# ScalarE's table loads written out around the Mish pairs, with every time of the issue order laid out anew

## The chip, the cores and the metric

One NeuronCore of a Trainium2 chip runs the kernel in one launch. The metric is device time in microseconds from one run to the next, as the median over runs; a profiled execution shows every instruction on TensorE (PE; its weight loads PEld), VectorE (DVE), ScalarE (ACT), GpSimd (POOL) and SyncE's queue (SP).

## The reference

Attention within clusters, and a feed-forward network with Mish behind it. Cut to what matters:

```python
# q, k, v: (4, 8, 768, 64); centroids: (8, 16, 64); w_in: (512, 2048); w_out: (2048, 512)
q_assign = argmax(q_n . c_n); k_assign = argmax(k_n . c_n)        # nearest of 16 centroids, per head
scores = where(q_assign == k_assign, q @ k.T / 8, -1e9)
attn = softmax(scores) @ v                                        # exp, row sum, divide
x = attn as (3072, 512)
h = x @ w_in
sp = where(h > 20, h, log1p(exp(min(h, 20))))
out = (h * tanh(sp)) @ w_out                                      # h * tanh(softplus(h)) is Mish
```

## The kernel before, in words

**Units.** The attention runs in 96 units: 32 heads (4 batches of 8) times 3 blocks of 256 query rows, and a unit in two halves `a` of 128 rows. One half goes through `scores` (s: four matmuls into two PSUM banks; two such tiles exist, so the scores two halves later need the exponential that reads these banks), `rowmax` (m, DVE), `expo` (p, ACT, with the row sum l), `total` and `recip` (l), `p_hi` (hl, POOL), `p_lo` (hl, DVE), `ptrans` (pt, a DMA that transposes, issued on SP). Two units are a pair: `pv` multiplies their pt with the values (o), `pv_out` copies the result on ACT (x) and `x_lo` on DVE makes its low part. The first 24 units have a form of their own, with transposes on TensorE (q, pt) and without a second table; meanwhile both weights are loaded and prepared (`w_load`, `w_abs`, `w_low`, `w_f32`, `w_sq`, then `w_hi`, `w_lo`).

**FFN.** It follows the attention by 24 units. With every pair of units run two steps j of the first product: `m1` (h, 2 parts of 12 matmuls), `e_mish` (u, ACT), `e_gh` (g, POOL), `e_gl` (g, DVE), and, for the tile of 256 rows that is complete, steps `m2(k, a, f)` of the second product (O, six matmuls each; step f needs g of j = 8k + f), then `m_out` (osb, ACT) and `m_store`. The steps j from 80 on are done another way at the end, from some 770 us on; their order is not touched.

**Operands.** Each head's q and k are loaded on SP (`qk_load`), split on POOL (`prep_hi`, `prep_lo`: A, B), copied by DMA or ACT (`copy_t`, `copy_z`, `copy_b`, `copy_a`: T, Z), and assigned to clusters for four heads at a time (`assign_mm`, `assign_turn`, `assign_max`, `assign_hot`, `assign_back`, `assign_put`, `assign_stg`, `hot_copy`). `v_load`, `v_sq`, `v_high`, `v_split` do the like for the values.

**The order.** Nothing is scheduled by readiness: each engine works in the order in which the steps are issued. Every step has a time, in units, made from the tables `T` and `N`; `Plan.run` issues the steps by their times, and a step first issues those it names with `after` when they have not been issued. So a step can be pulled ahead of its own time. For the units behind the 24th and the FFN the times are:

```python
e = i // 2 * 2 + N["E"][i % 2 * 2 + a]
for key in ("scores", "rowmax", "expo", "total", "recip", "p_hi", "p_lo", "ptrans"):
    pl.at(e + N[key], ops[key], i, a)
...
pl.at(i + N["x_lo"] + 0.1 * (u - i), x_lo, u)          # u = i - 1 and i, i odd
...
t = ffn(j // 2 * 2)                                    # 23.993 + the even one of j
pl.at(t + N["m1"][j % 2 * 2 + fi], m1, j, fi)
for key in ("e_mish", "e_gh", "e_gl"):
    pl.at(t + N[key][j % 2], ops[key], j)
...
pl.at(ffn(8 * k + 4 * a + f / 2 + N["m2"][8 * a + f]), m2, k, a, f)
```

Below, e48_0 is the exponential of unit 48's half 0, s, m and p_lo likewise, and x46 the copy of unit 46's output.

**Tables.** ScalarE looks functions up in one table set at a time; the exponential and Mish are in different sets. At the start line 105 loads a set with the exponential and the logarithm by hand; every other load was put in by the builder, ahead of the first function that the loaded set lacks.

Of the kernel before, what the change touches and what calls it, by code (L numbers as in the profile page):

```python
# [26 lines left out]
class Plan:  # L27
# [9 lines left out]
        self.state = {}  # L37

    def at(self, t, fn, *args):
        self.ops[fn.__name__, *args] = (t, len(self.ops), fn, args)  # L40

    def issue(self, op):
        if op not in self.state:
# [28 lines left out]
def tile_clustered_attention_mish_ffn(  # L72
# [9 lines left out]
    nc = tc.nc  # L82
# [748 lines left out]
    def e_mish(j):  # L831
        pl.after(("m1", j, 0), ("m1", j, 1))
        if j % 2 == 0:
            st["g", j // 2] = gp.tile([P, 2, 2, 512], F16, tag="g2", name=f"g{j // 2}", bufs=4)
        st["u", j] = mp.tile([P, 512], F32, tag="u", name=f"u{j}")
        nc.scalar.activation(st["u", j], st["h", j], AF.Mish, scale=vst[j // 24, "h"])  # L836

    def e_gh(j):
        pl.after(("e_mish", j))
        nc.gpsimd.tensor_scalar(  # L840
            st["g", j // 2][:, j % 2, 0], st["u", j], vst[j // 24, "g"], 1.0,
            op0=ALU.mult, op1=ALU.mult,
        )
# [226 lines left out]
    def ffn(j):  # L1070

        return T["ffn"] + j

    ops = {
        fn.__name__: fn
        for fn in (scores, rowmax, expo, total, recip, p_hi, p_lo, ptrans, e_mish, e_gh, e_gl)
    }
    def start(i):

        return N["u"][i] if i < 24 else i  # L1080
# [37 lines left out]
    for q, n in owner.items():  # L1118
        if q == 0:
            continue  # L1120
        t = -12 if q == 0 else start(first[n]) + 3 * T["assign"]
# [15 lines left out]
    for n in range(32):  # L1137
        p = n // 16
        t = N["w"][n]
# [5 lines left out]
    for i in range(16):  # L1145
        t = N["ws"][i]
# [3 lines left out]
    def half(key, n, op):  # L1150
        i, a = divmod(T[key] + n, 2)
        if mode(i, a) == 3:
            return start(i) + T[op, a]
        return i // 2 * 2 + N["E"][i % 2 * 2 + a] + N[op]

    for p in range(2):
        t = half(("wh", p), 0, "scores")
# [3 lines left out]
    for b in range(2):  # L1161
        t = half(("vh", b), 0, "scores")
# [47 lines left out]
    for j in range(80):  # L1210
        t = ffn(j // 2 * 2)
# [4 lines left out]
    for k in range(9):  # L1216
        for a in range(2):
            for f in range(8):
                pl.at(ffn(8 * k + 4 * a + f / 2 + N["m2"][8 * a + f]), m2, k, a, f)
            t = ffn(8 * k + 4 * a + 3.5 + N["m2"][8 * a + 7])  # L1220
# [7 lines left out]
    for f in range(8):  # L1228
        for op in (c_whole, c_sums, c_high, c_low):
            pl.at(us(T["tail", "c"][f] + T["c", op.__name__]), op, f)  # L1230
        t = 7.84 * f
# [5 lines left out]
    for n in range(16):  # L1237
        a, f = divmod(n, 8)
        t = 3.92 * n + 2.62
# [33 lines left out]
    ('vh', 0): 5,  # L1273
    ('vh', 1): 45,
    'vh_step': 1,
    'v_sqd': -1.793,
    'cent_put': -17.25,
    'ffn': 23.993,
    'w_f': 0.331,
    'w_q': 0.827,  # L1280
    'w_lo': 0.305,
    ('z', 'prep_hi'): -17.4,
    ('z', 'prep_lo'): -15.2,
    ('z', 'copy_t'): -17.3,
    ('z', 'copy_a'): -15.0,
    ('z', 'copy_b'): -15.01,
    ('z', 'copy_z'): -15.1,
    ('z', 'assign_mm'): -15.0,
    ('z', 'assign_turn'): -15.05,
    ('z', 'assign_max'): -14.9,  # L1290
    ('z', 'assign_hot'): -14.8,
    ('z', 'assign_back'): -14.7,
    ('z', 'assign_put'): -14.6,
    ('z', 'hot_direct'): -14.55,
    ('z', 'assign_stg'): -14.4,
    ('z1', 'prep_hi'): -16.637,
    ('z1', 'copy_t'): 0.652,
    ('z1', 'prep_lo'): -0.394,
    ('z1', 'copy_z'): 0.103,
    ('z1', 'copy_b'): 0.753,  # L1300
    ('z1', 'copy_a'): 0.423,
    'as_turn': 1.351,
    'as_max': -0.357,
    'as_hot': 4.283,
    'as_back': 0.815,
    'as_put': 1.374,
    'as_stg': 1.508,
    'n_late': 9,
    'wide': 24,
    'v_s0': 36.614,  # L1310
    'act_q': 3,
    'xbufs': (5, 7, 4),
    'v_sq': 20.406,
    'assign': -1.297,
    'hot_copy': -0.251,
    'copy_a': -0.21,
    'copy_b': -0.38,
    'copy_z': -0.725,
    'copy_t': -0.806,
    'prep_lo': 1.071,  # L1320
    'prep_hi': 3.185,
    'load': -3.206,
    'raw': 4,
    ('f_ws', 0): 0,
    ('f_ws', 1): 1,
# [22 lines left out]
    ('f_b', 1): 1,  # L1348
    ('f_l', 0): 0.096,
    ('f_l', 1): 1,  # L1350
    ('w_l', 0): 2.19,
    ('w_l', 1): 1.226,
    'v0': -19.148,
    'v_d': -1.18,
    ('q_hi', 0): 2.631,
    ('q_lo', 0): 0.521,
    ('q_trans', 0): 0.78,
    ('q_hi', 1): 0.793,
    ('q_lo', 1): 3.324,
    ('q_trans', 1): 1.225,  # L1360
    ('f_w', 0): 1,
    ('f_w', 1): 0.659,
    'units0': 24,
# [5 lines left out]
    'O': 1,  # L1369
    ('ws1', 0): 2.668,  # L1370
    ('ws1', 1): -3.407,
    ('scores', 0): -0.068,
    ('rowmax', 0): -0.01,
    ('expo', 0): 0.345,
    ('recip', 0): 2.622,
    ('scores', 1): 0.349,
    ('rowmax', 1): 0.599,
    ('expo', 1): 6.966,
    ('recip', 1): 1.335,
    'pv': 1.42,  # L1380
    'pv_step': 0.487,
    'v_scale': 0.114,
    'pv_out': 2.609,
    ('w_s', 0): -0.341,
    ('w_s', 1): -0.361,
    ('f_sh', 0): 0.995,
    ('f_sh', 1): 1,
}


N = {
    ('load', 0): -7.458,
    ('load', 1): -10.096,
    ('load', 2): -6.974,
    ('load', 3): -4.979,
    'prep_hi': -3.418,
    'prep_lo': 0.494,
    'copy_t': -2.17,
    'copy_z': -2.427,
    'copy_a': -1.038,  # L1400
    'hot_copy': -2.049,
    'copy_b': -1.075,
    'assign_mm': -4.285,
    'assign_turn': -1.043,
    'assign_max': -4.058,
    'assign_hot': 0.071,
    'assign_back': -3.503,
    'assign_put': -0.183,
    'assign_stg': -2.372,
    'v_load': 16.573,  # L1410
    'v_sq': 18.112,
    'v_scale': 21.77,
    'v_max': 22.2,
    'v_pair': 10,
    'v_high': 26.705,
    'v_low': 27.262,
    'v_d': 2.046,
    'E': [0.355, 0.767, 1.154, 1.513],
    'scores': 2.166,
    'rowmax': -0.272,  # L1420
    'expo': -0.103,
    'total': 6.164,
    'recip': 0.144,
    'p_hi': 11.217,
    'p_lo': 1.549,
    'ptrans': 0.865,
    'pv': [5.55, 13.269, 7.015],
    'pv_out': 6.881,
    'x_lo': 2.789,
    'm1': [0.368, 0.616, 0.939, 1.346],  # L1430
    'e_mish': [4.782, 1.75],
    'e_gh': [1.685, 3.448],
    'e_gl': [1.743, 2.41],
    'm2': [4.854, 4.854, 4.854, 4.854, 4.854, 4.854, 4.854, 4.854, 4.881, 4.881, 4.881, 4.881, 4.881, 4.881, 4.881, 4.881],
    'm_out': -0.431,
    'm_store': 0.376,
# [3 lines left out]
}  # L1440


# [26 lines left out]
```

## Time and profile before

| | us |
|---|---|
| runs | 907.83, 908.76, 910.4 |
| their median | 908.76 |
| span of the profiled execution, first to last instruction | 908.0 |
| busy: PE / DVE / ACT / POOL | 850.7 / 701.2 / 516.8 / 416.9 |
| table loads on ACT: 1 at line 105, 35 at line 659 (exponential), 36 at line 836 (Mish) | 1.283 each |

For the profiled execution only its span is given; the runs' times are of other executions. Busy shares are averages over stretches with different limits. Matmuls overlap and their ends are modelled, so a busy PE is not PE at its peak; a wait of PE counts here only as the time in which it has no matmul at all.

### The profile page before, as it was taken

The page shows a single profiled execution, that of the slowest core. Times are in us where ns is not written, and L with a number is a line of the kernel's source. Part 1 is how long each engine was busy: PE and PEld are TensorE (multiplying, and loading weights), DVE is VectorE, ACT ScalarE, POOL GpSimd, SP SyncE. Part 2 cuts the span into 40 slices and gives each one's busy share as a digit, 9 for nine tenths or more (in the row PEclk, how much of TensorE's full clock was granted, in tenths as well). Part 3 has the DMA queues.
Part 4 walks back from the last instruction along what each step waited for, and adds up shares of the span by engine and source line. Part 5 has one row for each costly group of instructions (what it writes and reads, how often), then busy time and mean ns, then how long its engine had stood idle before and what let it go on. Part 6 is the DMA issues. An engine that isn't in the chain of part 4 may idle for free.

```text
span 908.0 us, 17381 instructions
## 1 busy us (share of the span) xinstructions
PE 850.7 (94%) x6671; PEld 611.1 (67%) x6671; DVE 701.2 (77%) x1178; ACT 516.8 (57%) x876; POOL 416.9 (46%) x410
## 2 busy tenths in 40 slices
PE   7899788869999999899999999999999999999998
PEld 3666565656667666677667667667667676677787
DVE  7879978777897769788987689699887776378841
ACT  6767867655556565556565666556556565145520
POOL 1443638565556445456555455466555544110000
PEclk9999999999999999999999999999999999999999
DMA  8645582258677796679779787679587675200001
GB/s 326 209 142 161 161 243 59 48 100 170 127 152 156 145 241 117 116 159 182 142 136 173 186 178 144 121 152 197 113 137 150 140 143 93 48 12 12 2 19 41
DMA packets 253058, 121.49 MB, mean 134 GB/s; under 512 B 230288, under 2 KB 230800, under 8 KB 252976
## 3 DMA queue, kind: packets, MB, share of 16 engines
q1 hardware_dynamic: 247632, 108.46, 54.4%
q10 hardware_dynamic: 5344, 11.93, 6.2%
q8 instruction: 52, 0.85, 0.4%
q14 instruction: 30, 0.25, 0.1%
HBM read 35.72 MB, written 6.29 MB: 46 GB/s over the span
## 4 chain that ended last, share of the span: by engine, by line
PE 48%; DVE 22%; issue 9%; ACT 8%; POOL 7%; DMA 5%; ACTq 0%; SPq 0%; POOLq 0%; DVEq 0%
DVE m L647 6%; PE o L750 6%; PE h L827 5%; DVE hl L714 5%; PE h L828 5%; PE h L829 5%; PE s L630 4%; PE O L864 4%; PE O L866 4%; PE O L865 4%; PE s L635 4%; DVE g L848 4%; ACT p L659 3%; POOL g L840 2%; DMA pt<-hl 2%
## 5 line engine op out<-in xcount | busy, mean ns | idle before, releaser
L659 ACT ACTIVATE p<-s,m 128x768 f32<-128x768 f32 x192 | 173.0, 901 | 116.6 <-DVE l L671 89.9
L697 POOL TENSOR_SCALAR hl<-p,l 128x768 f16<-128x768 f32 x144 | 160.2, 1117 | 123.9 <-DVE l L679 43.3
L647 DVE TENSOR_REDUCE m<-s 128x1 f32<-128x768 f32 x192 | 182.4, 950 | 32.2 <-PE s L635 28.8
L714 DVE SCALAR_TENSOR_TENSOR hl<-p,l,hl 128x768 f16<-128x768 f32 x144 | 181.2, 1259 | 8.6 <-POOL hl L697 8.2
L827 PE MATMUL h<-x,w 128*128 128x256 f16 x640 | 176.9, 276 | 3.8 <-ACT u L836 3.6
L828 PE MATMUL h<-x,w 128*128 128x256 f16 x640 | 175.5, 274 | 0.0
L829 PE MATMUL h<-x,w 128*128 128x256 f16 x640 | 175.5, 274 | 0.0
L630 PE MATMUL s<-A,B 128*128 128x384 f32 x384 | 122.0, 399 | 19.9 <-ACT p L659 14.7
L840 POOL TENSOR_SCALAR g<-u,mscg 128x512 f16<-128x512 f32 x80 | 72.5, 906 | 143.6 <-ACT u L836 135.3
L866 PE MATMUL O<-w,g 128*128 128x512 f16 x320 | 121.4, 379 | 7.6 <-DVE g L848 7.6
L864 PE MATMUL O<-w,g 128*128 128x512 f16 x320 | 121.8, 381 | 2.8 <-POOL g L840 2.7
L865 PE MATMUL O<-w,g 128*128 128x512 f16 x320 | 121.3, 379 | 0.0
L635 PE MATMUL s<-Z,T 80*128 80x384 f32 x384 | 100.1, 342 | 0.7 <-DMA T<-stg 0.6
L827 PEld LDWEIGHTS <-w 128*128 128x128 f16 x768 | 75.5, 98 | 32.5 <-issue 21.8
L630 PEld LDWEIGHTS s<-A,B 128*128 128x128 f32 x384 | 62.9, 191 | 44.0 <-ACT p L659 24.3
L848 DVE SCALAR_TENSOR_TENSOR g<-u,mscg,g 128x512 f16<-128x512 f32 x80 | 83.9, 1049 | 9.2 <-POOL g L840 6.8
L659 ACT ACT_TABLE_LOAD x35 | 44.9, 1283 | 79.3 <-DVE m L647 72.1
L828 PEld LDWEIGHTS <-w 128*128 128x128 f16 x768 | 75.9, 99 | 14.9 <-issue 4.2
L829 PEld LDWEIGHTS <-w 128*128 128x128 f16 x768 | 75.5, 98 | 9.0
L750 PE MATMUL o<-pt,v 128*64 128x256 f16 x1296 | 78.1, 274 | 0.5 <-DVE l L671 0.5
L750 PEld LDWEIGHTS <-v 128*64 128x64 f16 x1296 | 67.7, 110 | 15.7 <-issue 12.4
L635 PEld LDWEIGHTS s<-Z,T 80*128 80x128 f32 x384 | 70.2, 190 | 1.5 <-DMA T<-stg 0.9
(225 smaller groups left out, 1311.5 us busy)
## 6 DMA issues: line engine op xcount, KB each, us to landing
qk<-in_qk_dram SPq DMA_DIRECT2D x32, 384.0 KB, 5.0
stage<-in_w_in_dram SPq DMA_DIRECT2D x16, 512.0 KB, 7.6
stage<-in_w_out_dram SPq DMA_DIRECT2D x16, 512.0 KB, 5.1
vraw<-in_vP_dram SPq DMA_DIRECT2D x16, 384.0 KB, 6.5
T<-A ACTq DMA_DIRECT2D x30, 192.0 KB, 3.2
Z<-B SPq DMA_DIRECT2D x30, 192.0 KB, 3.3
B<-T ACTq DMA_DIRECT2D x28, 192.0 KB, 3.7
out_dram<-osb SPq DMA_DIRECT2D x20, 256.0 KB, 4.4
```

The lines of the kernel that those rows point to most:

```text
L630: nc.tensor.matmul(s[:, j, :384], st["B", n][:, q0 : q0 + P], st["A", n][:, j * 384 : (j + 1) * 384], start=True, stop=False,)
L635: nc.tensor.matmul(s[:, j, :384], st["T", n][: D + NCL, q0 : q0 + P], st["Z", n][: D + NCL, j * 384 : (j + 1) * 384], start=False, stop=True,)
L647: nc.vector.tensor_reduce(m, st["s", i, a][:, :, :384], axis=AX.XY, op=ALU.max, negate=True)
L659: nc.scalar.activation(p.rearrange("p (n x) -> p n x", n=2), st["s", i, a][:, :, :384], AF.Exp, bias=st["m", i, a], scale=1.0, accum_out=l,)
L697: nc.gpsimd.tensor_scalar(t[:, 0], p, r, 1.0, op0=ALU.mult, op1=ALU.mult)
L714: nc.vector.scalar_tensor_tensor(t[:, 1], p, r, t[:, 0], op0=ALU.mult, op1=ALU.subtract)
L750: nc.tensor.matmul(o[s * D : s * D + D, :256], v if early else v[:, int(part == 1)], st["pt", 2 * m + s][:, :, c + (0 if early or part < 2 ...
L827: nc.tensor.matmul(o, wh, xh, start=(c == 0), stop=False)
L828: nc.tensor.matmul(o, wh, xl, start=False, stop=False)
L829: nc.tensor.matmul(o, wl, xh, start=False, stop=(c == 3))
L864: nc.tensor.matmul(o, gh, wh, start=(f == 0 and fi == 0), stop=False)
L866: nc.tensor.matmul(o, gl, wh, start=False, stop=(f == 7 and fi == 1))
```

## The change

`e_mish` gets two loads written out: Mish's set ahead of the first Mish of a pair, and the exponential's set behind the second one, for j below 72. `Plan.at` can add a shift to a step's time, from a table `SHIFT` that is empty. Nearly all times in `T` and `N` are new; no computation is added or left out. The diff, with the lists `u`, `w` and `ws` and most of `T` left out:

```diff
     def at(self, t, fn, *args):
-        self.ops[fn.__name__, *args] = (t, len(self.ops), fn, args)
+        op = fn.__name__, *args
+        self.ops[op] = (t + SHIFT.get(op, 0), len(self.ops), fn, args)
...
         st["u", j] = mp.tile([P, 512], F32, tag="u", name=f"u{j}")
+        if j % 2 == 0:
+            nc.scalar.preload_act_table_set("mish")
         nc.scalar.activation(st["u", j], st["h", j], AF.Mish, scale=vst[j // 24, "h"])
+        if j % 2 and j < 72:
+            nc.scalar.preload_act_table_set("natural_log_exp_and_others")
...
-    ('w_l', 0): 2.19,
-    ('w_l', 1): 1.226,
+    ('w_l', 0): 3.03,
+    ('w_l', 1): 0.965,
...
 N = {
-    ('load', 0): -7.458,
-    ('load', 1): -10.096,
-    ('load', 2): -6.974,
-    ('load', 3): -4.979,
-    'prep_hi': -3.418,
-    'prep_lo': 0.494,
-    'copy_t': -2.17,
-    'copy_z': -2.427,
+    ('load', 0): -9.013,
+    ('load', 1): -10.835,
+    ('load', 2): -6.827,
+    ('load', 3): -5.085,
+    'prep_hi': -3.572,
+    'prep_lo': 1.216,
+    'copy_t': -2.829,
+    'copy_z': -2.24,
...
-    'E': [0.355, 0.767, 1.154, 1.513],
-    'scores': 2.166,
-    'rowmax': -0.272,
-    'expo': -0.103,
-    'total': 6.164,
-    'recip': 0.144,
-    'p_hi': 11.217,
-    'p_lo': 1.549,
-    'ptrans': 0.865,
-    'pv': [5.55, 13.269, 7.015],
-    'pv_out': 6.881,
-    'x_lo': 2.789,
-    'm1': [0.368, 0.616, 0.939, 1.346],
-    'e_mish': [4.782, 1.75],
-    'e_gh': [1.685, 3.448],
-    'e_gl': [1.743, 2.41],
-    'm2': [4.854, 4.854, 4.854, 4.854, 4.854, 4.854, 4.854, 4.854, 4.881, 4.881, 4.881, 4.881, 4.881, 4.881, 4.881, 4.881],
-    'm_out': -0.431,
-    'm_store': 0.376,
+    'E': [0.382, 0.808, 1.235, 1.505],
+    'scores': 0.582,
+    'rowmax': -0.28,
+    'expo': 4.085,
+    'total': 9.597,
+    'recip': 0.209,
+    'p_hi': 11.057,
+    'p_lo': 1.167,
+    'ptrans': 0.814,
+    'pv': [6.978, 19.207, 5.531],
+    'pv_out': 8.853,
+    'x_lo': 2.778,
+    'm1': [0.136, 0.893, 1.132, 1.575],
+    'e_mish': [6.744, 1.671],
+    'e_gh': [1.774, 2.299],
+    'e_gl': [1.667, 2.915],
+    'm2': [4.545, 6.49, 7.882, 4.714, 5.842, 6.227, 6.493, 4.761, 4.932, 5.145, 5.769, 4.636, 4.154, 4.821, 7.994, 4.844],
+    'm_out': -0.422,
+    'm_store': 0.914,
...
+SHIFT = {
...
+}
```

## Rows read from the trace of the kernel before

**Rows 1.** Busy time by stretch: PE, PEld, DVE, ACT, POOL, then clock, DMA share, GB/s

```profile
0.00:187.00 187.00, 159.78 (x1169) 109.89 (x1170) 153.06 (x284) 131.06 (x253) 85.75 (x105) 0.99 0.55 166
187.00:240.00 53.00, 43.06 (x340) 31.89 (x342) 42.67 (x67) 29.53 (x48) 33.52 (x31) 0.94 0.75 146
240.00:770.00 530.00, 513.80 (x4072) 363.89 (x4064) 429.78 (x700) 307.64 (x501) 289.34 (x265) 1.00 0.76 150
770.00:908.00 138.00, 134.03 (x1096) 105.42 (x1096) 75.69 (x128) 48.55 (x76) 8.33 (x11) 1.00 0.08 22
```

**Rows 2.** PE's waits from 240 to 770: us in total, times, longest us

```profile
PE O L866 <- DVE g L848: 7.1, 14, 0.9
PE s L630 <- ACT p L659: 5.4, 8, 1.5
PE O L864 <- POOL g L840: 2.7, 4, 0.8
```

**Rows 3.** PE's waits from 187 to 240

```profile
PE s L630 <- ACT p L659: 6.9, 3, 4.3
PE h L827 <- ACT u L836: 3.0, 1, 3.0
```

**Rows 4.** ACT's groups, 240 to 770: busy us, mean ns | idle before, its releasers

```profile
L659 ACT ACTIVATE p<-s,m 128x768 f32<-128x768 f32 x128 | 115.2, 900 | 98.2 <-DVE l L671 81.4 <-DVE m L647 15.1
L836 ACT ACTIVATE u<-h,msch 128x512 f32<-128x512 f32 x65 | 44.3, 682 | 0.7
L659 ACT ACT_TABLE_LOAD x32 | 41.1, 1283 | 66.9 <-DVE m L647 59.7 <-DVE vsm L398 7.2
L836 ACT ACT_TABLE_LOAD x32 | 41.1, 1283 | 0.6
```

**Rows 5.** ACT's timeline in one pair: start us, us, instruction [idle before]

```profile
473.84 0.38 ACT L787 ACTIVATE x<-o 64x256 f16<-64x256 f32 x1 [0.66 <-PE o L750]
...
478.24 1.28 ACT L659 ACT_TABLE_LOAD   x1 [1.05 <-DVE m L647]
```

**Rows 6.** The chain of waits, 463 to 490: start us, us, what

```profile
463.73 1.28 ACT L659
465.02 1.00 ACT p L659 x2
466.07 0.62 PE s L630 x2
...
467.27 0.11 PE h L829
...
468.36 0.35 PE s L630 x2
...
471.69 2.09 PE o L750 x36
...
474.09 0.21 PE O L865
...
487.16 2.09 PE o L750 x36
```

**Rows 7.** DVE's groups, 240 to 770

```profile
L714 DVE SCALAR_TENSOR_TENSOR hl<-p,l,hl 128x768 f16<-128x768 f32 x128 | 160.4, 1253 | 6.3 <-POOL hl L697 6.0
L647 DVE TENSOR_REDUCE m<-s 128x1 f32<-128x768 f32 x128 | 121.7, 951 | 21.9 <-PE s L635 21.0
L848 DVE SCALAR_TENSOR_TENSOR g<-u,mscg,g 128x512 f16<-128x512 f32 x66 | 70.8, 1073 | 2.1
L811 DVE SCALAR_TENSOR_TENSOR x<-o,x 64x256 f16<-64x256 f32 x52 | 22.0, 422 | 48.5 <-ACT x L787 47.4
```

**Rows 8.** ACT's waits from 120 to 132: us in total, times, longest us

```profile
ACT pt L728 <- DMA Z<-B: 3.1, 1, 3.1
```

**Rows 9.** The tile pt, 200 to 770: its DMAs, issue to landing

```profile
DMA to landing us min/median/max: 3.6/3.9/8.0
```

**Rows 10.** ACT's groups over the whole span: the load at line 105

```profile
L105 ACT ACT_TABLE_LOAD x1 | 1.3, 1283 | 1.7 <-PEq L1459 1.7
```

More of the change, by code (lines that the diff above doesn't have):

```diff
@@ L1275 @@
     'vh_step': 1,
-    'v_sqd': -1.793,
-    'cent_put': -17.25,
+    'v_sqd': -5.865,
+    'cent_put': -16.698,
     'ffn': 23.993,
-    'w_f': 0.331,
+    'w_f': 0.342,
     'w_q': 0.827,
[L1281 to L1307, printed above, removed]
+    'w_lo': 0.312,
+    ('z', 'prep_hi'): -17.672,
+    ('z', 'prep_lo'): -12.698,
+    ('z', 'copy_t'): -15.888,
+    ('z', 'copy_a'): -14.732,
+    ('z', 'copy_b'): -14.765,
+    ('z', 'copy_z'): -16.337,
+    ('z', 'assign_mm'): -11.552,
+    ('z', 'assign_turn'): -14.554,
+    ('z', 'assign_max'): -16.003,
+    ('z', 'assign_hot'): -13.258,
+    ('z', 'assign_back'): -12.666,
+    ('z', 'assign_put'): -12.998,
+    ('z', 'hot_direct'): -6.027,
+    ('z', 'assign_stg'): -14.77,
+    ('z1', 'prep_hi'): -15.822,
+    ('z1', 'copy_t'): -0.562,
+    ('z1', 'prep_lo'): -2.335,
+    ('z1', 'copy_z'): 2.134,
+    ('z1', 'copy_b'): 2.571,
+    ('z1', 'copy_a'): 1.339,
+    'as_turn': 2.548,
+    'as_max': -0.442,
+    'as_hot': 2.486,
+    'as_back': 0.39,
+    'as_put': 0.846,
+    'as_stg': 1.187,
     'n_late': 9,
     'wide': 24,
-    'v_s0': 36.614,
+    'v_s0': 36.503,
     'act_q': 3,
     'xbufs': (5, 7, 4),
[L1313 to L1322, printed above, removed]
+    'v_sq': 20.248,
+    'assign': -1.284,
+    'hot_copy': -0.423,
+    'copy_a': -0.208,
+    'copy_b': -0.408,
+    'copy_z': -0.702,
+    'copy_t': -0.829,
+    'prep_lo': 0.852,
+    'prep_hi': 0.614,
+    'load': -4.519,
     'raw': 4,
@@ L1350 @@
     ('f_l', 1): 1,
-    ('w_l', 0): 2.19,
-    ('w_l', 1): 1.226,
[L1353 to L1360, printed above, removed]
+    ('w_l', 0): 3.03,
+    ('w_l', 1): 0.965,
+    'v0': -18.341,
+    'v_d': -5.322,
+    ('q_hi', 0): 4.355,
+    ('q_lo', 0): 0.677,
+    ('q_trans', 0): 0.738,
+    ('q_hi', 1): 0.764,
+    ('q_lo', 1): 4.007,
+    ('q_trans', 1): 1.215,
     ('f_w', 0): 1,
@@ L1371 @@
     ('ws1', 1): -3.407,
[L1372 to L1376, printed above, removed]
+    ('scores', 0): -0.149,
+    ('rowmax', 0): 0.082,
+    ('expo', 0): 0.31,
+    ('recip', 0): 3.8,
+    ('scores', 1): 0.364,
     ('rowmax', 1): 0.599,
[L1378 to L1381, printed above, removed]
+    ('expo', 1): 3.986,
+    ('recip', 1): 1.374,
+    'pv': 1.419,
+    'pv_step': 0.48,
     'v_scale': 0.114,
-    'pv_out': 2.609,
-    ('w_s', 0): -0.341,
-    ('w_s', 1): -0.361,
+    'pv_out': 2.608,
+    ('w_s', 0): 0.187,
+    ('w_s', 1): -0.515,
     ('f_sh', 0): 0.995,
@@ L1391 @@
 N = {
-    ('load', 0): -7.458,
-    ('load', 1): -10.096,
-    ('load', 2): -6.974,
-    ('load', 3): -4.979,
-    'prep_hi': -3.418,
-    'prep_lo': 0.494,
-    'copy_t': -2.17,
-    'copy_z': -2.427,
[L1400 to L1411, printed above, removed]
+    ('load', 0): -9.013,
@@ L1412 @@
+    ('load', 1): -10.835,
[5 more added lines that the diff above has]
+    'copy_z': -2.24,
+    'copy_a': -2.094,
+    'hot_copy': -1.531,
+    'copy_b': -0.948,
+    'assign_mm': -4.206,
+    'assign_turn': -3.351,
+    'assign_max': -3.982,
+    'assign_hot': 1.536,
+    'assign_back': -3.3,
+    'assign_put': 0.576,
+    'assign_stg': -2.392,
+    'v_load': 17.344,
+    'v_sq': 18.153,
     'v_scale': 21.77,
-    'v_max': 22.2,
+    'v_max': 21.48,
@@ L1414 @@
     'v_pair': 10,
-    'v_high': 26.705,
-    'v_low': 27.262,
-    'v_d': 2.046,
-    'E': [0.355, 0.767, 1.154, 1.513],
-    'scores': 2.166,
-    'rowmax': -0.272,
-    'expo': -0.103,
-    'total': 6.164,
-    'recip': 0.144,
-    'p_hi': 11.217,
-    'p_lo': 1.549,
-    'ptrans': 0.865,
-    'pv': [5.55, 13.269, 7.015],
-    'pv_out': 6.881,
-    'x_lo': 2.789,
-    'm1': [0.368, 0.616, 0.939, 1.346],
-    'e_mish': [4.782, 1.75],
-    'e_gh': [1.685, 3.448],
-    'e_gl': [1.743, 2.41],
-    'm2': [4.854, 4.854, 4.854, 4.854, 4.854, 4.854, 4.854, 4.854, 4.881, 4.881, 4.881, 4.881, 4.881, 4.881, 4.881, 4.881],
@@ L1435 @@
-    'm_out': -0.431,
-    'm_store': 0.376,
[3 rows of a table removed]
+    'v_high': 26.765,
+    'v_low': 27.613,
+    'v_d': 3.411,
+    'E': [0.382, 0.808, 1.235, 1.505],
[14 more added lines that the diff above has]
+    'e_gl': [1.667, 2.915],
```

6 rows, old and new, of the table N are left out of this document.

## The prediction

> **What bounds the kernel now.** I read the busy time by stretch first, cut at the first Mish load (187 us), at 240 and at 770, where the last pairs of units end [rows 1]. From 240 to 770 TensorE is busy 513.80 of 530.00 us with a granted clock of 1.00, while DVE has 429.78 and ScalarE 307.64: TensorE is the bound, and 16.2 us is what its idle time can give back. From 187 to 240 it idles 9.94 us of 53, before 187 it idles 27.2 us, after 770 only 4.0.
>
> Then TensorE's own waits. Between 240 and 770 they are 5.4 us of scores waiting for an exponential (8 times), and 7.1 + 2.7 us of the second FFN product waiting for g [rows 2]. Between 187 and 240 they are 6.9 us for three exponentials and 3.0 us for a Mish [rows 3].
>
> Then ScalarE. From 240 to 770 it loads a table 64 times at 1283 ns: 32 times for the exponential (line 659), with 66.9 us of idle time ahead of them, and 32 times for Mish (line 836), with 0.6 us ahead [rows 4]. So the exponential's load stands behind its instruction's wait for the row maximum: at 478.24 ScalarE has idled 1.05 us for m, and only then loads [rows 5]. The Mish's load does not wait for the matmul that its Mish waits for; it costs 1.28 us between an exponential and a Mish. The chain of waits shows the price where it counts: load at 463.73, exponential at 465.02, and the scores that need that exponential's banks start at 466.07 [rows 6].
>
> **The exponential's load behind the second Mish.** It waits for nothing there, so it leaves the path m, load, exponential. It saves the smaller of 1.28 us and the idle time in front of it: 66.9 / 32 is 2.1 us on average, so nearly always the whole 1.28. Mish's load written out stays where it was, behind an exponential. Five loads are added: Mish's for the four pairs from j = 72 on (three of them with no exponential between), and an exponential's behind the pair before. They are 5 x 1.283 = 6.4 us of ScalarE, at or after the last exponential, where it is busy 48.55 of 138 us [rows 1]: I cost them at nothing, and at 6.4 us if that cover were gone.
>
> The order around them decides the rest. I worked it out from the times and from what each step pulls forward. For a pair of units 48, 49 (Mish 24, 25) ScalarE had: e48_0, e48_1, e49_0, e49_1, load, Mish, x46, Mish, x47, load, e50_0. It gets: e48_0, e48_1, e49_0, load, Mish, Mish, load, x46, e49_1, x47, e50_0. So the Mish pair and both loads move ahead of the pair's fourth exponential, and that exponential moves behind the copy x46, which waits for the pair's P·V product.
>
> From the end of P·V to the end of e50_0, before: x 0.38, x_lo 0.42, g 1.07, x_lo 0.42, p_lo 1.25, row maximum 0.95, load 1.28, exponential 1.00, in all 6.77 [rows 4 to 7]. The trace agrees: P·V ends at 471.69 + 2.09 = 473.78, and the load at 478.24 puts the exponential's end at 480.54. After: x 0.38, e49_1 1.00, x 0.38, x_lo 0.42, p_lo 1.25, row maximum 0.95, exponential 1.00, in all 5.38; g now stands ahead of x_lo, where P·V covers it. So e50_0 ends 1.4 us sooner against P·V.
>
> What queues behind. The second load ends 0.68 + 1.28 = 1.96 us after the second Mish's matmuls. TensorE has P·V's 2.09 us behind these, in one pair of four also one FFN step of 6 x 0.215 = 1.3 us: the copy x46 has 0.1 or 1.4 us to spare, and where an earlier exponential was late, it starts late. The fourth exponential ends 1.38 us after P·V; the scores that take its banks start 2.0 us after P·V at the soonest (scores 4 x 0.17, then 12 x 0.11) [rows 6]. Its p_lo stood behind the next row maximum and still does, so the transposes go out about when they did: that p_lo starts 4.5 us after P·V before, 4.4 after. On SyncE's queue loads of q and k move ahead of some transposes; each waits for a buffer that, by the order, an earlier step has freed. GpSimd gets the odd g ahead of the fourth p_hi, 0.7 to 1.4 us of work that ends before that exponential does.
>
> TensorE's order is less even: the FFN steps in four pairs were 3, 5, 3, 5 and are 1, 7, 2, 6, several of them right behind P·V. A pair's third scores come 5.3 us after P·V in the shortest kind (9 of 36), 7.9 or more in the others; they need e50_0 at 5.38. Before they came about 8.0 after, against 6.77. So three kinds of four gain spare time, and the shortest has none.
>
> **Sum, 240 to 770.** The 5.4 us of scores: seven of the eight waits follow a loaded exponential and are (5.4 - 1.5) / 7 = 0.56 us on average, less than the 1.28 taken out; the eighth, 1.5 us, has the odd g ahead of a row maximum on DVE, and that g moves behind it. All 5.4; the bounds are 0 and 5.4. The 9.8 us for g: Mish is one exponential (1.00) sooner, and two more FFN steps (2.6 us) lie ahead of the ones that waited, but the odd g now stands behind e49_1 and the second x: 0.38 + 1.00 + 0.38 + 0.42 + 1.07 = 3.25 us after P·V against 3.9 for its matmul. If the load is a microsecond late, it waits again. I take two thirds, 6.5; the bounds are 0 and 9.8. New waits in the shortest pairs: half a microsecond in some, 2. Together 9.9.
>
> **187 to 240.** Pairs without second products are shorter than the loop, so each of three waits loses up to 1.28: about 3.0 of 6.9 [rows 3]. The Mish that TensorE waits 3.0 us for is one exponential sooner, 1.0. Together 4.0. The granted clock is 0.94 here, a mean over both levels [rows 1]; what shorter waits give back of it is at most 0.06 x 53 = 3.2, and I count nothing.
>
> **Before 187.** No table is loaded there; the moves are many and small. One has a row: ScalarE waits 3.1 us for Z<-B [rows 8], a transfer queued on SyncE behind four weight loads, and now behind three. I take 2.4. The bounds are a loss of 5 and a gain of 8, about a fifth and a third of the idle 27.2.
>
> 9.9 + 4.0 + 2.4 = 16.3. The profiled span is 908.0, and the median of the runs is 0.8 above it: 908.8 - 16.3 = 892.5. Waits are counted as idle time only, and a matmul's end is modelled late (they start 0.11 us apart, rows 6, while each counts as longer), so the true loss is a little larger: 891.
>
> A load is one row of 1283 ns, and in the trace before, 32 Mish loads have 0.6 us of idle time ahead of them in all [rows 4], and at 463.73 + 1.28 the exponential follows its load at once [rows 6]: two written loads cost 2.57 us and no more. The Trainium skill, page "ScalarE: Activation LUTs", section "What ACT_TABLE_LOAD costs", states the same 1283 ns and adds a drain of about 1380 ns to every switch. The trace agrees with the load and shows no room for the drain; by it the two loads of a pair would hold ScalarE 2.76 us longer.
>
> **Rivals.**
> Only the load leaves the path, and the moves give and take alike: seven waits, 3.9 us, and 3.0 from 187 to 240, so 902. For it: 9.8 us of the gain hang on g, whose order changes both ways. Against: e50_0 gains on the whole loop.
>
> No change: TensorE, 97% busy from 240 to 770, hides the loads, and the early moves lose what the loads gain: 906 to 911. Against it stand the waits of rows 2 and 3.
>
> Slower: the fourth exponential now depends on P·V, so P·V, exponential, p_hi, p_lo, transposes, next P·V become one loop: 0.38 + 1.00 + 0.38 + 0.42 + 1.25 + 0.95 + 1.25 = 5.63, a transpose's landing 3.9 (at most 8.0) [rows 9], P·V 2.09, in all 11.6. Half of the pairs shrink to 14.0 us between P·V products (15.47 before: 471.69 to 487.16) [rows 6]. From a landing above 6.3 us the next product is late, and the lateness is handed on. At 1.5 us in 18 pairs this is 27 us, so 891 + 27 = 918. For it: landings reach 8.0. Against: the median is 3.9.
>
> Loads that cost double, because each must wait for what ScalarE has under way: priced at one more load row each, 2.57 us for the two, x46 is 2.57 - 0.1 = 2.5 us late in the short pairs. The 9 shortest have nothing to spare and lose it: 22 us, so 891 + 22 = 913. Rows 4 and 6 speak against it. The skill's drain, named above, is this case; its own figure would give 2.76 - 0.1 = 2.7 in 9 pairs, about 915.
>
> The builder adds its own loads to the written ones: then the exponential pays 1.28 again, and the time is 905 to 912. Against it: the load at line 105 is written out, and line 187's exponential has no load of its own [rows 10].
>
> **Numbers.** Forecast 0.62 (range 879 to 898); only the load 0.16; no change 0.07; slower by the loop 0.11; loads that cost double 0.02; loads added twice 0.02. The forecast's lower end takes back all 25.1 us of rows 2 and 3, the 2.4 and the clock's 3.2, less a microsecond: 879. Its upper end is g at 0 gain: 898. For 8 in 10 the range goes up to 908, through the second case and half of the third. Faster by over 0.3% (what a measurement of this kernel can tell from no change) 0.79, within it 0.08, slower 0.13.
>
> **What would show it.** Right: no idle time ending in a load at an exponential; two loads per pair around two neighbouring Mish; PE's waits on exponentials from 240 to 770 under 1 us; waits on g at most 4; the stretch between two P·V products uneven, 14 to 18 us, with a mean under 15.6. Wrong: P·V waiting for a transpose, x46 starting a microsecond or more behind P·V's end, the first scores after Mish waiting for the fourth exponential, or an early part that ends later than 187.

## The result, and the profile after

The changed kernel takes 881.25 us (median of 4 runs, 878.82 to 882.74) beside 909.18 for the kernel before (907.83 to 910.40): a ratio of 0.9685, 95% interval 0.9658 to 0.9711. Run again beside the last experiments it took 879.21 (6 runs, 877.55 to 880.75), 0.9662 [0.9636, 0.9687]. It is faster by 28 to 30 us, where 18 were forecast; the time lies in the forecast's range.

To see where the time came from, both traces have to be cut at the same work, not at the same microsecond. I cut them where the exponential of the first half of units 24, 30 and 90 starts. These are landmarks on ScalarE; on TensorE, whose order changed, up to 31 matmuls fall on another side of them. Busy time by stretch, cut there, first before and then after; the columns are those of [rows 1].

```profile
0.00:175.24 175.24, 148.15 (x1075) 101.25 (x1076) 145.74 (x271) 124.79 (x242) 82.01 (x103) 0.99 0.56 172
175.24:231.12 55.88, 46.23 (x352) 34.32 (x352) 43.35 (x67) 29.80 (x48) 34.18 (x31) 0.94 0.62 121
231.12:725.68 494.56, 479.30 (x3804) 339.44 (x3803) 405.21 (x657) 287.66 (x469) 273.49 (x249) 1.00 0.77 154
725.68:908.00 182.32, 176.99 (x1443) 136.08 (x1441) 106.90 (x186) 74.54 (x119) 27.26 (x28) 1.00 0.22 47
```

```profile
0.00:166.37 166.37, 145.71 (x1084) 100.19 (x1086) 145.60 (x270) 124.66 (x243) 77.85 (x101) 1.00 0.60 183
166.37:212.56 46.19, 39.49 (x321) 29.23 (x322) 39.26 (x65) 29.72 (x48) 36.53 (x32) 1.00 0.74 142
212.56:696.09 483.53, 480.88 (x3820) 342.69 (x3819) 406.98 (x659) 286.57 (x468) 293.75 (x251) 1.00 0.82 157
696.09:878.40 182.31, 177.66 (x1449) 136.98 (x1447) 109.67 (x186) 80.99 (x124) 27.94 (x29) 1.00 0.23 47
```

The four stretches shrink by 8.9, 9.7, 11.0 and 0.0 us, in all 29.6. In each, the stretch's length less TensorE's busy time (the two figures behind the stretch's bounds) is TensorE's idle time: it falls from 27.1 to 20.7, from 9.7 to 6.7, from 15.3 to 2.7, and from 5.3 to 4.7, by 22.7 in all. The other 6.9 us are busy time, for the same matmuls (6671 in the first trace, 6670 in the second). Most of it goes between units 24 and 30, where each matmul is shorter at the higher clock and 31 fewer fall. These 31 lie in the other stretches now; at the 0.13 us of busy time that one has there before (46.23 / 352), some 4 of that stretch's 9.7 us moved and weren't saved.

TensorE's waits after, from 220 to 740 us (total, times, longest), against [rows 2]. The second FFN product never waits for g any more, and two waits for an exponential are left of eight:

```profile
PE s L631 <- ACT p L660: 1.5, 2, 1.0
PE o L751 <- DMA pt<-hl: 0.7, 1, 0.7
PE as L543 <- DMA qk<-in_qk_dram: 0.2, 1, 0.2
```

The two waits for an exponential have a new cause. Both exponentials stand behind a cast on ScalarE (line 512) that waits for a transfer; from 240 to 770 us before, that cast has only 0.4 us of idle time ahead of it. ScalarE's waits over the same stretch have:

```profile
ACT A L512 <- DMA T<-A: 6.7, 2, 3.7
```

ScalarE's groups over the same stretch, against [rows 4]. The exponential's load (line 841) now has 0.6 us of idle time ahead of it in all, where it had 66.9: it no longer stands behind a wait.

```profile
L660 ACT ACTIVATE p<-s,m 128x768 f32<-128x768 f32 x129 | 115.9, 898 | 140.0 <-DVE l L672 71.5 <-DVE m L648 68.2
L839 ACT ACTIVATE u<-h,msch 128x512 f32<-128x512 f32 x66 | 42.6, 685 | 4.0 <-PE h L830 3.6
L841 ACT ACT_TABLE_LOAD x33 | 42.3, 1283 | 0.6
L838 ACT ACT_TABLE_LOAD x32 | 41.1, 1283 | 0.6
```

One pair on ScalarE's timeline, against [rows 5]. By the count of exponentials it is the pair of units 58 and 59, as there; x46, x47 and e50_0 name the places in the order. In the chain of waits its P·V product is the row `448.03 2.09 PE o L751 x36`, so it ends at 450.12. Load, two Mish and load lie ahead of that, x46 starts 0.06 us behind it, the fourth exponential and x47 follow, and e50_0 starts at 454.77, behind its row maximum alone.

```profile
445.48 1.28 ACT L838 ACT_TABLE_LOAD   x1
446.77 0.69 ACT L839 ACTIVATE u<-h,msch 128x512 f32<-128x512 f32 x1
448.06 0.69 ACT L839 ACTIVATE u<-h,msch 128x512 f32<-128x512 f32 x1 [0.60 <-PE h L830]
448.77 1.28 ACT L841 ACT_TABLE_LOAD   x1
450.18 0.38 ACT L788 ACTIVATE x<-o 64x256 f16<-64x256 f32 x1
450.46 0.88 ACT L660 ACTIVATE p<-s,m 128x768 f32<-128x768 f32 x1
...
451.46 0.38 ACT L788 ACTIVATE x<-o 64x256 f16<-64x256 f32 x1
...
454.77 0.90 ACT L660 ACTIVATE p<-s,m 128x768 f32<-128x768 f32 x1 [1.24 <-DVE m L648]
```

### The profile page after: what moved, and what is told of

The parts are those of the page before. It is cut to its first block, busy times and chain, and to the rows that moved or that the text cites. A ratio compares the mean times of both kernels' runs of the same rounds, so it can differ in the third digit from the quotient of the medians.

```text
span 878.4 us, 17434 instructions
## 1 busy us (share of the span) xinstructions
PE 843.7 (96%) x6670; PEld 609.1 (69%) x6671; DVE 701.5 (80%) x1178; ACT 521.9 (59%) x881; POOL 436.1 (50%) x410
## 4 chain that ended last, share of the span: by engine, by line
PE 71%; DVE 12%; DMA 6%; ACT 6%; issue 3%; POOL 2%; ACTq 0%; SPq 0%; POOLq 0%; DVEq 0%
PE o L751 9%; PE h L828 8%; PE h L830 7%; PE h L829 7%; PE O L869 7%; PE O L871 7%; PE O L870 7%; PE s L631 5%; PE s L636 5%; DVE m L648 3%; ACT p L660 2%; DMA T<-A 2%; DVE hl L715 2%; DMA stage<-in_w_out_dram 1%; PE as L543 1%
## 5 line engine op out<-in xcount | busy, mean ns | idle before, releaser
L698 POOL TENSOR_SCALAR hl<-p,l 128x768 f16<-128x768 f32 x144 | 174.8, 1214 | 135.9 <-DVE l L680 68.8
L715 DVE SCALAR_TENSOR_TENSOR hl<-p,l,hl 128x768 f16<-128x768 f32 x144 | 166.8, 1159 | 7.7 <-POOL hl L698 7.5
L631 PE MATMUL s<-A,B 128*128 128x384 f32 x384 | 119.2, 391 | 8.9 <-ACT p L660 6.8
L853 DVE SCALAR_TENSOR_TENSOR g<-u,mscg,g 128x512 f16<-128x512 f32 x80 | 93.6, 1170 | 38.6 <-POOL g L845 38.3
L751 PE MATMUL o<-pt,v 128*64 128x256 f16 x1296 | 78.4, 274 | 1.6 <-DMA pt<-hl 1.3
L631 PEld LDWEIGHTS s<-A,B 128*128 128x128 f32 x384 | 61.1, 190 | 25.1 <-ACT p L660 10.5
L751 PEld LDWEIGHTS <-v 128*64 128x64 f16 x1296 | 68.1, 110 | 11.9 <-issue 9.3
L839 ACT ACTIVATE u<-h,msch 128x512 f32<-128x512 f32 x80 | 51.8, 685 | 16.8 <-PE h L830 12.5
```

What stands on the lines that cost most here:

```text
L631: nc.tensor.matmul(s[:, j, :384], st["B", n][:, q0 : q0 + P], st["A", n][:, j * 384 : (j + 1) * 384], start=True, stop=False,)
L715: nc.vector.scalar_tensor_tensor(t[:, 1], p, r, t[:, 0], op0=ALU.mult, op1=ALU.subtract)
L751: nc.tensor.matmul(o[s * D : s * D + D, :256], v if early else v[:, int(part == 1)], st["pt", 2 * m + s][:, :, c + (0 if early or part < 2 ...
```

## The experiments

All kernels compute the whole reference. The theory was the prediction's: the load goes off the path, and the order around it makes room for it. For each kernel the table gives its median time, its ratio to the kernel before beside it with the 95% interval, and, from its own trace, the us spent up to unit 24, from unit 24 to 30, from 30 to 90 and behind 90.

```
kernel             median  ratio [95%]               <24    24-30  30-90  >90
before             909.2                             175.2  55.9   494.6  182.3
early_order        903.3   0.9935 [0.9910, 0.9959]   168.9  53.7   496.1  182.3
loads_alone        921.0   1.0136 [1.0110, 1.0161]   177.7  54.0   504.0  185.8
load_behind_copy   903.5   0.9929 [0.9907, 0.9952]   176.7  51.5   491.3  183.5
order_alone        887.0   0.9751 [0.9728, 0.9775]   166.9  48.8   489.6  179.8
late_order_loads   890.2   0.9806 [0.9771, 0.9840]   177.6  46.1   481.1  182.3
after              881.3   0.9685 [0.9658, 0.9711]   166.4  46.2   483.5  182.3
after_beside       879.2   0.9662 [0.9636, 0.9687]   168.1  46.2   482.3  182.3
fourth_exp_first   910.9   1.0020 [1.0002, 1.0039]   171.6  50.2   506.8  183.1
two_more_loads     932.9   1.0259 [1.0225, 1.0292]   167.9  54.6   523.3  186.3
even_ffn_steps     885.5   0.9732 [0.9702, 0.9762]   168.0  48.8   482.9  183.9
odd_g_early        883.2   0.9709 [0.9676, 0.9742]   169.2  46.8   483.9  184.7
no_spare_loads     878.4   0.9657 [0.9626, 0.9688]   169.4  46.2   485.1  180.7
no_spare_again     877.2   0.9644 [0.9617, 0.9671]   166.0  46.2   482.5  180.7
```

### The written loads without the order

```
 # the order of the kernel before, and
+        if j % 2 == 0:
+            nc.scalar.preload_act_table_set("mish")
         nc.scalar.activation(st["u", j], st["h", j], AF.Mish, ...)
+        if j % 2 and j < 72:
+            nc.scalar.preload_act_table_set("natural_log_exp_and_others")
```

> The order of before with the two loads written out and nothing else. On ScalarE the exponential's load then stands behind the second Mish and ahead of the second x copy. Theory: a loaded exponential no longer pays 1.28 us behind its row maximum, so the seven waits of scores from 240 to 770 (3.9 us) go and three waits from 187 to 240 lose 1.28 or less each (3.0 us): about 902 us, and the waits for g stay near 9.8 us. Rival 1: TensorE hides the loads anyway and the new order alone makes the time: 908 to 910. Rival 2: the load holds up the second x copy, and with it DVE: 910 or more.

It took 921.0, 12 us slower: the theory of a gain fell, and the second rival (the load holds up the second copy, 910 or more) was right. ScalarE's timeline in one pair, then VectorE's:

```profile
476.59 0.69 ACT L839 ACTIVATE u<-h,msch 128x512 f32<-128x512 f32 x1
477.23 0.38 ACT L788 ACTIVATE x<-o 64x256 f16<-64x256 f32 x1
477.51 0.67 ACT L839 ACTIVATE u<-h,msch 128x512 f32<-128x512 f32 x1
478.20 1.28 ACT L841 ACT_TABLE_LOAD   x1
479.49 0.38 ACT L788 ACTIVATE x<-o 64x256 f16<-64x256 f32 x1
```

```profile
479.90 0.43 DVE L812 SCALAR_TENSOR_TENSOR x<-o,x 64x256 f16<-64x256 f32 x1 [0.43 <-ACT x L788]
480.36 1.36 DVE L715 SCALAR_TENSOR_TENSOR hl<-p,l,hl 128x768 f16<-128x768 f32 x1
481.75 0.96 DVE L648 TENSOR_REDUCE m<-s 128x1 f32<-128x768 f32 x1
```

In the old order the second Mish stands between the two copies, so a load directly behind it comes ahead of the second copy. VectorE works in the order of issue: x_lo waits for that copy, and p_lo and the row maximum stand behind x_lo. Most of the 1.28 us is still on the path to e50_0 (from the end of P·V to the end of e50_0 it is a mean of 7.64 us from 235 to 745 us, against 8.06 before), and it now holds up p_lo too. TensorE's waits for g from 240 to 780 us are 16.4 us, against 9.8 in [rows 2]:

```profile
PE O L871 <- DVE g L853: 9.7, 13, 1.4
PE O L869 <- POOL g L845: 6.7, 6, 1.6
```

Not all of the 12 us is the load's place: five more loads are run here than before (77 against 72), and behind unit 90 the profile is 3.5 us longer (185.8 against 182.3).

### The order without the written loads

```
 # the changed kernel, without
-        if j % 2 == 0:
-            nc.scalar.preload_act_table_set("mish")
-        if j % 2 and j < 72:
-            nc.scalar.preload_act_table_set("natural_log_exp_and_others")
```

> The new order without the written loads; the builder puts the exponential's load ahead of the fourth exponential of a pair, behind the first x copy. Theory: the fourth exponential, the second x copy and the next pair's first exponential each come up to 1.28 us later against P.V; pairs with few FFN steps have nothing to spare, 9 to 18 pairs at about 1.3 us, so 893 to 902 us. Rival: the order alone makes the gain, and the loads are hidden wherever they stand: 880 to 884.

It took 887.0, between the two expectations: the order brings 22 of the 28 us by itself, and the written loads the last 6 (8 against the changed kernel's second measurement). The builder's own load lands here behind x46, ahead of the fourth exponential, one place from where the change writes it:

```profile
453.48 0.38 ACT L788 ACTIVATE x<-o 64x256 f16<-64x256 f32 x1 [1.43 <-PE o L751]
453.88 1.28 ACT L660 ACT_TABLE_LOAD   x1
455.17 0.90 ACT L660 ACTIVATE p<-s,m 128x768 f32<-128x768 f32 x1
...
456.19 0.38 ACT L788 ACTIVATE x<-o 64x256 f16<-64x256 f32 x1
```

ScalarE idles 1.43 us for P·V ahead of x46: that is the idle time in which the written load lies in the changed kernel. This kernel has 74 loads: the new order itself needs two more than the old one's 72.

### The load behind the second copy, in the old order

```
 # the order of the kernel before; in the copy of unit i:
             nc.scalar.activation(x[...], o[...], AF.Copy, ...)
+            if i % 2 and i <= 91:
+                nc.scalar.preload_act_table_set("natural_log_exp_and_others")
```

> The order of the kernel before, with the exponential's load written directly behind the second x copy of a pair (the last thing that ScalarE does before it waits for the row maximum), and no load of Mish's written. Theory: the load is then hidden behind the wait for the row maximum (idle time 2.1 us ahead of the load before) and holds up no copy, so that the path loses up to 1.28 us a pair in the pairs that wait: about 902, 899 to 905. Rival: the load isn't what the path waits for in the old order: 907 to 910.

It took 903.5, as the theory had it: 17.5 us below `loads_alone`. Not all of that is the place, one copy later, since the five more loads are gone too. Between units 24 and 90, where the order and the number of loads are the same, the profiles take 558.0 and 542.8 us, and 550.4 before: the place is worth some 15 us, half of it loss and half of it gain. The timeline shows it between the copy and the wait for the row maximum:

```profile
471.25 0.38 ACT L787 ACTIVATE x<-o 64x256 f16<-64x256 f32 x1
471.65 1.28 ACT L789 ACT_TABLE_LOAD   x1
...
475.18 0.90 ACT L659 ACTIVATE p<-s,m 128x768 f32<-128x768 f32 x1 [1.55 <-DVE m L647]
```

From the end of P·V to the end of e50_0 it is a mean of 6.79 us here, less than the changed kernel's 6.90. But units 30 to 90 take 491.3 us, and 483.5 there: shortening this path alone does not make the change's gain.

### The fourth exponential back ahead of Mish

```
-    'expo': 4.085,
+    'expo': 0.135,
```

> The changed kernel with one time of the order moved: the exponential of a pair's fourth half goes back ahead of the pair of Mish and both loads on ScalarE, instead of behind copy x46. Theory: the exponential's load still hides ahead of x46, only Mish and what follows it (g) come some 1.1 us later and the copies x46 and x47 up to 1.1 us: 883 to 888. Rival 1: what makes the gain is that the exponential stands behind x46, where its load comes for nothing; without it the exponential waits for its scores and holds up Mish: over 890. Rival 2: its place is worth nothing: 880.5 to 882.

It took 910.9: all of the gain is gone, and the theory with its 883 to 888 fell; the first rival's side (over 890) was right: the exponential holds up Mish. ScalarE's timeline in one pair, then VectorE's:

```profile
483.19 0.90 ACT L660 ACTIVATE p<-s,m 128x768 f32<-128x768 f32 x1 [1.05 <-DVE l L672]
...
484.20 1.28 ACT L838 ACT_TABLE_LOAD   x1
485.49 1.27 ACT L839 ACTIVATE u<-h,msch 128x512 f32<-128x512 f32 x2
486.77 1.28 ACT L841 ACT_TABLE_LOAD   x1
488.07 0.38 ACT L788 ACTIVATE x<-o 64x256 f16<-64x256 f32 x1
```

```profile
487.00 1.38 DVE L853 SCALAR_TENSOR_TENSOR g<-u,mscg,g 128x512 f16<-128x512 f32 x1 [2.71 <-POOL g L845]
488.48 0.42 DVE L812 SCALAR_TENSOR_TENSOR x<-o,x 64x256 f16<-64x256 f32 x1
```

The time that was changed is that of all four halves, but on ScalarE only the fourth exponential changes its place. The whole block of load, two Mish and load (3.83 us) now starts behind the fourth exponential. x46 starts a median of 2.37 us behind the end of P·V (30 products from 235 to 745 us), against 0.34 in the changed kernel (32 products). VectorE waits 2.71 us for that Mish's g, with x_lo, p_lo and the row maximum behind it. On the path from P·V to e50_0 the exponential's place behind x46 saves nothing (it adds its own time there); it lets the block start one exponential sooner, and so fit under P·V.

### Two more loads in the block

```
             nc.scalar.preload_act_table_set("natural_log_exp_and_others")
+            nc.scalar.preload_act_table_set("mish")
+            nc.scalar.preload_act_table_set("natural_log_exp_and_others")
```

> The changed kernel with two more loads (Mish's, then the exponential's again) behind every written exponential's load, 2.57 us more of ScalarE between the second Mish and the second pair of x copies. Theory, by the prediction's bound of the cover: copy x46 starts 0.5 us behind the end of the product P.V now, so all but some tenths of the 2.57 us come out in the path from P.V to the next units' exponentials, in each of the 35 or so periods whose spare is smaller than that; if TensorE has no other work in store for it, the nine shortest pairs alone lose 2.5 each, and the time is about 903, at least 895. Rival: the load is hidden behind P.V with room to spare, and TensorE, 99% busy between 220 and 740 us, has work in store: 882 to 885.

It took 932.9, on the theory's side, but 30 us beyond its 903. ScalarE's groups from 240 to 740 us:

```profile
L838 ACT ACT_TABLE_LOAD x29 | 37.2, 1283 | 0.5
L841 ACT ACT_TABLE_LOAD x29 | 37.2, 1283 | 0.5
L842 ACT ACT_TABLE_LOAD x29 | 37.2, 1283 | 0.2
L843 ACT ACT_TABLE_LOAD x29 | 37.2, 1283 | 0.2
```

The 2.57 us are plain loads without any gap between them. x46 starts a median of 2.53 us behind P·V, and the 30 pairs from unit 30 to 90 take 17.44 us each instead of 16.12: 1.3 of the 2.57 are lost in the average pair. By the four kinds of pair it is 1.4, 1.3, 0.7 and 1.9, not 2.5 in one kind and nothing in three. The block has too little cover left for them in any kind.

### The second product's steps made even

```
-    'm2': [4.545, 6.49, 7.882, 4.714, 5.842, 6.227, 6.493, 4.761, ...],
+    'm2': [4.854, 4.854, 4.854, 4.854, 4.854, 4.854, 4.854, 4.854, 4.881, ...],
```

> The changed kernel with the second product's times of the order put back to the even ones of before (steps per pair 3, 5, 3, 5 instead of 1, 7, 2, 6). Theory: the uneven steps are what keeps the second product from coming ahead of its g, with Mish in its new place too: waits of TensorE on g between 220 and 740 us come back, from none to 3 to 6 us, and the time is 885 to 889. Rival: Mish, which starts right behind the third exponential now, brings g in time by itself: no waits on g, 880 to 883.

It took 885.5, as the theory had it, and the waits on g are back, here from 220 to 740 us:

```profile
PE O L871 <- DVE g L853: 6.4, 8, 1.6
```

But they cost less than they last. Units 30 to 90 take 482.9, as in the changed kernel (482.3 and 483.5), with 12 fewer matmuls; units 24 to 30 take 48.8 against 46.2, with 14 more. Over both together it is 531.6 us. The changed kernel's two profiles have 529.7 and 528.5, and the two without the last loads of Mish, which differ from it only later, 531.2 and 528.7. So 6.4 us of waits cost 0 to 3 there; behind unit 90 it is 1.6 more (183.9 against 182.3). A gain that offsets part of the waits is not ruled out: with the even steps x46 never starts half a microsecond behind P·V, and in the changed kernel it does in 15 of 32 pairs.

### The odd g ahead of the row maximum

```
-    'e_gl': [1.667, 2.915],
+    'e_gl': [1.667, 2.41],
```

> The changed kernel with one time put back: the second g of a pair stands on VectorE ahead of the second half's row maximum again, not behind the next one. Theory: its 0.73 us then lies on the path row maximum, exponential, sum, p, transposes in the pairs that wait for it: 883 to 888, and waits of TensorE for scores or transposes show between 220 and 740 us. Rival: VectorE has idle time ahead of that row maximum, and g there costs nothing: 880 to 883.

It took 883.2 (881.35 to 886.31), at the edge of the theory's 883 to 888, and 4 above the changed kernel beside it (877.55 to 880.75); the intervals of the two ratios overlap, so the size stays open. The waits for scores grow as the theory said, from 1.3 in the run beside it to

```profile
PE s L631 <- ACT p L660: 4.0, 6, 1.4
```

### The two halves of the order

```
 # early_order: the kernel before with the new tables T, u, w and ws; no written loads
 # late_order_loads: the changed kernel with the old tables T, u, w and ws
```

> The code of before (no written loads) with the new times of the first 24 units alone (table T, and the times of units, weight loads and weight scaling); the later times are those of before. Theory: the 24th unit's first exponential starts 8.9 us sooner, as it does between the two traces, and the gain lasts to the end: about 900 us. Rival: the later part is bound by its own loop and takes the early gain back in part: 903 to 909.

> The written loads and the new times of all that follows the first 24 units, with the early times of before. Theory: the whole change but its early 8.9 us: about 890 us, with the waits of scores and g from the 30th unit on nearly gone as in the changed kernel. Rival: early and late part need each other, and the time is above 895.

The early tables alone bring 6 us (903.3, in the rival's band and not at the theory's 900); taken out of the changed kernel they cost 9 to 11 (890.2, the theory's 890, against 881.3 and 879.2). In the ten profiles with the new early tables unit 24 starts between 166.0 and 171.6 us, mean 168.2; in the four with the old ones between 175.2 and 177.7, mean 176.8. So the early part is worth 8.6, with a scatter of some 2 us from profile to profile.

### The last loads of Mish left out

```
-        if j % 2 == 0:
+        if j % 2 == 0 and j < 74:
             nc.scalar.preload_act_table_set("mish")
```

> The changed kernel, with Mish's load written only ahead of the pairs up to the 74th Mish; the last three, behind which no exponential comes, are left out. Theory: those three loads of 1.28 us are not covered, since the last Mish stand on the path to the end (TensorE idles 1.48 us ahead of one of the last second multiplications of the first product there, against 0.58 before): that idle time falls to about 0.6 and the kernel takes 0.5 to 1.5 us less than the changed one beside it, about 880. Rival: the loads hide there as well, and the time stays within 0.3 us of the changed kernel's 881.3.

> The changed kernel itself, as it is, beside the others: 881 (878 to 883) by every theory.

> The changed kernel without Mish's last three written loads, again, beside the changed kernel itself and with more rounds. Theory, from the profile of the first time (no idle time ahead of the last second multiplications, where the changed kernel has 1.48 us): 0.5 to 1.5 us below the changed kernel beside it. Rival: the two are within 0.4 us of each other.

It took 878.4 and 877.2, 2 to 3 us below the changed kernel's median each time, where 0.5 to 1.5 was expected. The single runs overlap (876.78 to 878.83 against 877.55 to 880.75 beside it), so the times alone do not settle the size. The traces do better: the part behind unit 90 takes 180.7 in both, against 182.3 in both of the changed kernel. In `order_alone`, which has the same 74 loads as the kernel without the three, it takes 179.8, but with 6 matmuls fewer behind that landmark (1443 against 1449). TensorE's wait in the changed kernel, from 740 us on, is not in the trace without the three loads:

```profile
PE h L828 <- ACT u L839: 1.5, 1, 1.5
```

## Why the prediction was right

**The direction and its ground held.** The load behind a wait became a load that nothing waits for, and its idle time went from 66.9 us to 0.6. But `loads_alone` shows that the writing by itself does not do it: written behind the second Mish in the old order, the same load makes the kernel 12 us slower. It needs the order's moves.

**From P·V to e50_0.** The sum had 6.77 us before and 5.38 after, 1.4 less. Over all products from 235 to 745 us the two traces have a mean of 8.06 and 6.90, 1.16 less, with the shortest at 6.48 and 5.55. The difference was about right; both sums lacked work that VectorE does in between in many pairs (V's scaling, a longer p_lo). But this path alone does not carry the gain: `load_behind_copy` has it at 6.79, and its units 30 to 90 take 7.8 us longer.

**x46's spare time** was put at 0.1 or 1.4 us. x46 starts a median of 0.34 us behind P·V's end, some half a microsecond or more in 15 of 32 pairs and a microsecond or more in 2. So the nothing to spare was right, in half of the pairs a little too hopeful, and it is the finest point of the change: `fourth_exp_first` and `two_more_loads` make x46 2.4 to 2.5 us late and lose 30 and 52 us.

**The uneven steps** take the waits on g away, as said (9.8 to 0, 6.5 forecast). But in the sum they stood as 6.5 us of gain, and `even_ffn_steps` shows that 6.4 us of these waits cost 0 to 3 between units 24 and 90. The prediction read from TensorE's busy share that TensorE was the bound, and took its idle time as gain one for one. The chain of work that ended last says otherwise; here are its shares by engine over the whole span, before and then after (what released a step is inferred):

```profile
PE 48%; DVE 22%; issue 9%; ACT 8%; POOL 7%; DMA 5%; ACTq 0%; SPq 0%; POOLq 0%; DVEq 0%
PE 71%; DVE 12%; DMA 6%; ACT 6%; issue 3%; POOL 2%; ACTq 0%; SPq 0%; POOLq 0%; DVEq 0%
```

Before, TensorE had less than half of this chain, and VectorE, ScalarE and GpSimd together 37%: work that passes between the engines set the pace in much of the kernel. After, most of it is TensorE's own, with even steps too (72%). Between units 30 and 90 alone, added up from the chain's pieces, TensorE's share goes from 39 to 83%. In `fourth_exp_first` and `two_more_loads`, whose x46 comes late, it is TensorE's at 40 and 29%.

**The terms of the sum.** From 240 to 770: 9.9 forecast, 12.6 us of idle time gone between units 30 and 90. From 187 to 240: 4.0 forecast; the waits for exponentials and Mish there fell from 9.9 to 5.7, 4.2 less, and all idle time between units 24 and 30 by 3.0. Before 187: 2.4 forecast, 6.4 gone; this term was taken from one transfer's row. That transfer's 3.1 us [rows 8] are no longer among ScalarE's waits, and TensorE's waits for the first exponentials (10.2 to 6.5 us) and for A and the staged rows (2.3 and 2.8 us to 0 and 0.5) fell too, while one for the weights grew (2.0 to 4.8); which move did it is not shown. Behind unit 90: nothing forecast, 0.7 gone. Busy time: 1.5 forecast, 6.9 gone, the largest error; the higher clock is a part of it, and the rest is not explained. Together 17.8 against 29.6. The direction was reasoned; that the time still lies within the range, near its lower end, is in part luck, since the two terms that went furthest past the forecast, busy time and the stretch before 187, were the least worked out: an allowance of 1.5 us, and one transfer.

**The added loads at nothing: wrong.** ScalarE is busy only 48.55 of 138 us there, but a share says nothing of the place: TensorE waits for one of the last Mish, and a load ahead of it is not covered. Three of the five cost 1.6 us, against the 6.4 given for no cover of all. The other two the new order needs anyway (the builder puts them in `order_alone`), and no run takes them away.

**The rivals.** "Only the load" at 902 was right for a load that is hidden (903.5), and wrong for the load where the change writes it, ahead of the copy (921.0). The slower loop through the fourth exponential did not come: transposes still land in 3.6 to 9.8 us, but TensorE waits for one once, 0.7 us. Loads added twice did not come: 77 in all, 72 plus five. Loads that cost double did not come. The Trainium skill, page "ScalarE: Activation LUTs", section "What ACT_TABLE_LOAD costs", has a drain of about 1380 ns with each switch to a different set. Here 116 loads in `two_more_loads` have 1.4 us of idle time ahead of them in all, and the trace disagrees with a drain. That rival's price was far too low all the same: it let only the 9 shortest pairs lose.

**What was to show it.** No load at an exponential's wait, two loads around two neighbouring Mish, waits on g under 4: all there. Waits on exponentials under 1: 1.5. P·V products 14 to 18 us apart with a mean under 15.6: 24 of 31 distances are, from 14.19 on, but two are over 20 us, and the pairs take 16.12 in the mean. The bound was wrong from the start, since it took one distance of 15.47 for the loop's pace, and the mean before was 16.49. Of the signs of being wrong two show, both small: P·V waits for a transpose once (0.7 us), and x46 starts a microsecond late in 2 of 32.

## What to carry to other kernels

A table load is a fixed piece of ScalarE's time (1283 ns in every run here); what matters is what stands behind it in the queues, its own engine's and those that wait for it. Put it behind the last thing that another engine needs soon, or under a product that ScalarE waits for anyway, and look at which copy it moves past: one place made some 15 us here, and one exponential's place 30. Compare two orders at the same work, not at the same time, and do not price idle time of TensorE as gain without asking, in the chain of work that ended last, which engines set the pace.

## What was not expected of the hardware

The granted clock between units 24 and 30 was 0.94 before (a mean over both of its levels) and 1.00 after, which looks like a cause. In the last run without the spare loads it is 0.93 in the same stretch:

```profile
165.97:212.19 46.22, 41.65 (x321) 30.96 (x322) 39.28 (x65) 29.73 (x48) 36.60 (x32) 0.93 0.73 141
```

The same 321 matmuls are busy 41.65 us instead of 39.49, and the stretch takes 46.22 instead of 46.19: the time came out of TensorE's idle time. In this stretch of this kernel the lower clock costs nothing, and the busy time that the changed kernel lost here is, in the part that the clock makes, no gain of its own.
